# Scores of three batches from float16 halves, and a plain float32 mix over the sequence, in an attention and mixer kernel

## The chip, the cores and the metric

The kernel runs on one core of a Trainium2 chip. Its time is the device time of one execution in microseconds. Before the change the median of three runs is 691.39 us (687.16 to 692.56).

## What is computed

The reference is attention with rotary positions followed by a mixer, for 4 batches, 8 heads, 576 positions and 64 numbers a head:

```python
q_rot, k_rot = (rotate(q), rotate(k))
scores = scale * np.matmul(q_rot, k_rot.transpose(0, 1, 3, 2))
scores = scores - np.max(scores, axis=-1, keepdims=True)
attn = np.exp(scores)
attn = attn / (np.sum(attn, axis=-1, keepdims=True) + 1e-09)
x = np.matmul(attn, v)            # heads side by side: (4, 576, 512)
h = x.transpose(0, 2, 1) @ U @ V  # over the sequence: 576 -> 32 -> 576
u = x + h.transpose(0, 2, 1)
out = u + np.maximum(u @ w_ch1, 0.0) @ w_ch2   # 512 -> 2048 -> 512
```

All arrays are float32.

## The kernel before

Heads are taken in pairs (`hp`, four of them a batch): a pair's 2 x 64 numbers fill the 128 rows of a tile. For each pair `load_qk` (L814) fetches q and k, each with a copy whose halves are swapped, into one of three `raw` buffers, and `rope` (L823) multiplies by the tables `cs` or `csq` and adds the two parts into a float32 tile of `qk_ring`.

A pair has five tiles of scores (`score_tiles`, L844). In the first four, 128 positions of each of the two heads are multiplied with all 576 keys: the two heads lie on rows 0 to 63 and 64 to 127, so that each head's matmul uses one half of TensorE's rows, and the four matmuls (two heads, two stretches of 288 keys) stand in one group. The fifth tile takes the last 64 positions of both heads at once from `ql`, a tile with zeros outside the two diagonal blocks, and uses all 128 rows. There are two score buffers, `s0` and `s1`, of two PSUM banks each.

`softmax_tile` (L870) takes the minimum of the negated scores on DVE (`nb`), the exponential on ACT, and for all but two pairs of batch 0 a high float16 half `p16` on ACT and a low one on POOL, which a transfer transposes into `pt`. `values` (L910) multiplies these with the float16 halves of v (`vh`, `vl`, `vb`), divides by the sum (`xt`), transposes into `x`, and for batches 1 to 3 splits the tile into two rounded parts, `xh` (a copy, then a subtraction).

When two pairs are done, `mix` (L989) forms U^T x: for batches 1 to 3 as ten float32r matmuls of `ust` with the two parts of `xh`, for batch 0 as five plain float32 matmuls of `uf` with the tiles `xfs`. Then it multiplies by V and adds to `x`.

The mixer (`mlp`, L1210) of batch b runs beside the attention of batch b + 1. But for the first half of batch 0, both its products are float16: for each of two halves of the positions 192 matmuls `mm<-u,wt` and 192 `mm<-room,wt`, in two PSUM banks; ACT and DVE split the hidden values into float16 halves in `room`. The mixer of batch 3 is left for the end.

The order of all this is not the order of the code. Every call is a node of `Plan`, which knows what it reads and writes; `cost` (L127) prices a call, `place` chooses an engine where a call has several ways, and `schedule` lays the nodes out forward and backward and keeps the shortest layout. The instructions are emitted in that order, so each engine's queue is fixed when the kernel is built.

## Time and profile before

| | us |
|---|---|
| median of three runs | 691.39 |
| lowest and highest | 687.16, 692.56 |
| profiled execution | 687.07 |
| its span, first to last instruction | 685.3 |
| PE busy in the span | 646.4 |
| DVE busy | 407.1 |
| ACT busy | 365.9 |
| POOL busy | 268.4 |

PE is TensorE's matmuls, PEld its weight loads, DVE VectorE, ACT ScalarE, POOL GpSimd and SP the queue of the transfers. The profile shows one execution; its time is shorter than the median of the runs. Names such as `mm<-u,wt` tell the tile written and the tiles read. All instructions are emitted from one line (L310), so the groups are told apart by tiles. A float32 matmul has two records in the trace. The duration of a matmul is that of one in a pipeline: where matmuls follow each other, the time from one start to the next is shorter than the duration, and the chain gives such stretches.

### The profile page before, as it was taken

The page shows a single profiled execution, that of the slowest core. Times are in us where ns is not written, and L with a number is a line of the kernel's source. Part 1 is how long each engine was busy: PE and PEld are TensorE (multiplying, and loading weights), DVE is VectorE, ACT ScalarE, POOL GpSimd, SP SyncE. Part 2 cuts the span into 40 slices and gives each one's busy share as a digit, 9 for nine tenths or more (in the row PEclk, how much of TensorE's full clock was granted, in tenths as well). Part 3 has the DMA queues.
Part 4 walks back from the last instruction along what each step waited for, and adds up shares of the span by engine and source line. Part 5 has one row for each costly group of instructions (what it writes and reads, how often), then busy time and mean ns, then how long its engine had stood idle before and what let it go on. Part 6 is the DMA issues. An engine that isn't in the chain of part 4 may idle for free.

```text
span 685.3 us, 14779 instructions
## 1 busy us (share of the span) xinstructions
PE 646.4 (94%) x5792; PEld 489.4 (71%) x5792; DVE 407.1 (59%) x1031; ACT 365.9 (53%) x817; POOL 268.4 (39%) x220
## 2 busy tenths in 40 slices
PE   2799986999998999999999999999999999999998
PEld 1577764677766677776777777777777777777776
DVE  4989777878887755656645663665555553430210
ACT  3766564449889766437644764447545652220210
POOL 1411356113447766565447545256444341000000
PEclk9999699999999999999999999999999999999999
DMA  7979889275377567447765576166854463000000
GB/s 227 327 242 295 238 153 175 88 226 143 99 162 129 123 107 149 100 122 167 172 104 142 103 160 113 57 167 112 140 96 80 87 114 62 18 1 27 10 10 27
DMA packets 178342, 86.90 MB, mean 127 GB/s; under 512 B 152032, under 2 KB 167520, under 8 KB 178272
## 3 DMA queue, kind: packets, MB, share of 16 engines
q1 hardware_dynamic: 178272, 85.96, 54.2%
q8 instruction: 45, 0.74, 0.4%
q14 instruction: 25, 0.20, 0.1%
HBM read 41.70 MB, written 4.72 MB: 68 GB/s over the span
## 4 chain that ended last, share of the span: by engine, by line
PE 74%; DVE 8%; DMA 6%; ACT 5%; POOL 3%; issue 3%; SPq 0%; POOLq 0%; ACTq 0%; DVEq 0%
PE mm L310 53%; PE s L310 13%; PE pv L310 8%; DMA pt<-p 5%; DVE wt L310 3%; ACT junk L310 2%; DVE junk L310 2%; ACT p L310 1%; POOL raw L310 1%; POOL p L310 1%; DMA cs<-tab 1%; DVE rs L310 1%; DMA raw<-qk 1%; ACT wt L310 1%; ACT room L310 1%
## 5 line engine op out<-in xcount | busy, mean ns | idle before, releaser
L310 PEld LDWEIGHTS <-wt 128*128 128x128 f16 x2688 | 257.0, 98 | 75.3 <-issue 12.7
L310 POOL TENSOR_TENSOR p<-p,p 128x576 f16<-128x576 f32 x120 | 162.0, 1365 | 162.3 <-ACT p L310 112.4
L310 PE MATMUL mm<-room,wt 128*128 128x288 f16 (+1 forms) x1472 | 213.9, 297 | 0.0
L310 PE MATMUL mm<-u,wt 128*128 128x288 f16 x1344 | 180.9, 286 | 3.1 <-DVE room L310 3.0
L310 DVE TENSOR_SCALAR_CACHE_REDUCE junk<-s 128x576 bf16<-128x576 f32 x144 | 104.9, 752 | 62.0 <-PE s L310 59.6
L310 ACT ACTIVATE p<-s,nb 128x576 f32<-128x576 f32 x144 | 103.2, 740 | 47.7 <-DVE junk L310 45.0
L310 ACT ACTIVATE room<-mm 128x288 f16<-128x288 f32 (+3 forms) x139 | 56.5, 411 | 111.8 <-PE mm L310 111.0
L310 PE MATMUL s<-qk,qk 64*128 64x288 f32 x512 | 87.7, 452 | 11.1 <-DVE qk L310 10.9
L310 DVE SCALAR_TENSOR_TENSOR room<-mm,room 128x288 f16<-128x288 f32 x112 | 50.7, 455 | 74.6 <-ACT room L310 73.8
L310 PEld LDWEIGHTS <-pt 128*128 128x128 f16 x1722 | 66.4, 98 | 26.5 <-DMA pt<-p 13.3
L310 ACT ACTIVATE p<-p 128x576 f16<-128x576 f32 x120 | 78.9, 682 | 4.1 <-DMA pt<-p 3.5
L310 PEld LDWEIGHTS s<-qk,qk 64*128 64x128 f32 x512 | 49.7, 196 | 30.8 <-DVE qk L310 10.9
L310 PE MATMUL pv<-vh,pt 128*128 128x65 f16 (+2 forms) x600 | 58.8, 204 | 4.5 <-DMA pt<-p 4.3
L310 PE MATMUL pv<-vl,pt 128*128 128x64 f16 (+2 forms) x600 | 58.4, 204 | 0.0
L310 ACT ACTIVATE xt<-pv,rc 128x64 f32<-128x64 f32 (+1 forms) x99 | 26.7, 311 | 57.5 <-DVE rc L310 52.2
L310 DVE SCALAR_TENSOR_TENSOR ob<-mm,so,x 128x288 f32<-128x288 f32 x28 | 14.4, 516 | 45.1 <-PE mm L310 45.1
L310 PE MATMUL mm<-x,wt 128*128 128x288 f32 x128 | 34.8, 423 | 1.9 <-ACT room L310 1.1
L310 PE MATMUL pv<-vb,pt 128*128 128x65 f16 (+1 forms) x448 | 33.3, 197 | 0.1
L310 DVE SCALAR_TENSOR_TENSOR wt<-wt 128x512 int32<-128x512 int32 x46 | 33.2, 755 | 0.0
L310 POOL TENSOR_TENSOR raw<-raw,csq 128x1152 f32<-128x1152 f32 x9 | 24.5, 2728 | 21.0 <-DMA raw<-qk 9.5
L310 DVE TENSOR_SCALAR rs<-pv,sc_v 128x2 f32<-128x2 f32 x63 | 13.8, 218 | 30.2 <-PE pv L310 29.5
L310 PEld LDWEIGHTS mm<-x,wt 128*128 128x128 f32 x128 | 23.9, 194 | 9.8 <-DVE x L310 1.5
(149 smaller groups left out, 673.3 us busy)
## 6 DMA issues: line engine op xcount, KB each, us to landing
raw<-qk SPq DMA_DIRECT2D x30, 576.0 KB, 4.3
wt<-w SPq DMA_DIRECT2D x23, 512.0 KB, 4.8
out_t<-ob SPq DMA_DIRECT2D x32, 144.0 KB, 1.8
x<-w SPq DMA_DIRECT2D x6, 512.0 KB, 4.3
raw<-vt SPq DMA_DIRECT2D x6, 512.0 KB, 4.1
pt<-p SPq DMA_TRANSPOSE x120, 3.3
vb<-vh SPq DMA_DIRECT2D x6, 264.0 KB, 3.3
u<-w SPq DMA_DIRECT2D x3, 512.0 KB, 3.5
```

The lines of the kernel that those rows point to most:

```text
L310: getattr(getattr(nc, eng), op)(*a, **k)
```

## The change

For batches 1 to 3 (`b >= FB`), `half_scales` finds for each head pair a power of two for q and one for k from their sums of squares, and `rope` writes each scaled tile as a high and a low float16 half into the bytes where the float32 tile stood. `score_tiles` adds three products (high x high, high x low, low x high) in PSUM, still with two heads on the two halves of the rows. `softmax_tile` undoes the scales: in the minimum, in `nb` and in the exponential's scale, which now come from memory. `mix` uses the plain float32 matmuls of batch 0 for all batches, and `values` writes the tiles `xfs` at once; `ust` and `xhs` go. `cost` prices a group of twelve float16 matmuls on 64 rows at half.

```diff
 class Plan.cost
-                    us += max(m, 64) * (4 if a[2].dtype == F32R and m < 256 else 1) / 2400
+                    k = 2 if list(a[1].ap)[0][1] <= 64 and len(calls) == 12 else 1
+                    us += max(m, 64) * (4 if a[2].dtype == F32R and m < 256 else 1) / 2400 / k
...
+    ql_ring = cycle([cst.tile([P, 2, P], F16, name=f"qh{i}") for i in range(2)])
...
-    ust = cst.tile([P, NC, 4 * R], F32R, name="ust")
-    uf = carve(NC * 4 * R, F32).rearrange("p (c r) -> p c r", c=NC)
-    xfs = [carve(2 * P, F32).rearrange("p (c d) -> p c d", c=2) for t in range(NC)]
+    uf = cst.tile([P, NC, 4 * R], F32, name="uf")
+    xfs = [cst.tile([P, 2, P], F32, name=f"xf{t}") for t in range(NC)]
-    xhs = [cst.tile([P, 2, 2, P], F32R, name=f"xh{t}") for t in range(NC)]
...
+        if b >= FB:
+            half_scales(b, hp)
+
+    def half_scales(b, hp):
+        sq = tmp("sqk", [2], 2, "")
+        for x in (1, 0):
+            nc.scalar.activation(
+                out=junks[2], in_=state[b, hp]["raw"][x][:, 0], func=AF.Square,
+                accum_out=sq[:, x:x + 1],
+            )
+        pb = bank("")
+        nc.tensor.matmul(pb[:, 0:2], ones, sq, start=True, stop=True)
+        a = tmp("aqk", [2], 2, "")
+        nc.vector.tensor_scalar(
+            out=a.bitcast(I32), in0=pb[:, 0:2].bitcast(I32), scalar1=24, scalar2=23,
+            op0=ALU.logical_shift_right, op1=ALU.logical_shift_left,
+        )
+        inv, sc = tmp("iqk", [2], 2, ""), tmp("cqk", [2], 2, "")
+        nc.vector.tensor_scalar(
+            out=inv, in0=a, scalar1=2.0**-126, scalar2=2.0**(64 - 15), op0=ALU.max, op1=ALU.mult,
+        )
+        nc.vector.reciprocal(out=sc, in_=inv)
+        both = tmp("bqk", [3], 2, "")
+        for o, x, f in ((0, inv, 1.0), (1, inv, -1.0), (2, sc, LOG_PSC)):
+            nc.vector.tensor_scalar(
+                out=both[:, o:o + 1], in0=x[:, 0:1], scalar1=x[:, 1:2], scalar2=f,
+                op0=ALU.mult, op1=ALU.mult,
+            )
...
     def rope(b, hp, x):
...
+        if b >= FB:
+            sc = state[b, hp]["sc"][0][:, x:x + 1]
+            two(r[:, 0], r[:, 0], r[:, 1], ALU.add, "DP")
+            hi, lo = [qk_[x].bitcast(F16)[:, i * S:(i + 1) * S] for i in range(2)]
+            nc.scalar.activation(out=hi, in_=r[:, 0], func=AF.Copy, scale=sc)
+            scaled_low(lo, r[:, 0], sc, hi, "DP")
...
+            return
         two(qk_[x], r[:, 0, :], r[:, 1, :], ALU.add, "DP")
...
     def score_tiles(b, hp, t):
...
+                with nc.group():
+                    for j, (x, y) in enumerate(((0, 0), (0, 1), (1, 0))):
+                        for n in range(2):
+                            hs = slice(n * HS, (n + 1) * HS)
+                            for e, s in enumerate(ss):
+                                own = slice(0, P) if t == NT else slice(e * 64, e * 64 + 64)
+                                nc.tensor.matmul(
+                                    half(s, n),
+                                    lw[:, x] if t == NT else qw[own, x, t * P:(t + 1) * P],
+                                    kw[own, y, hs], start=j == 0, stop=j == 2,
+                                )
...
     def softmax_tile(b, hp, s, dst, sm):
...
-                    out=next(unread) if len(parts) == 1 else next(unread)[:, 0], in0=i, scalar1=0.0 if plain else LOG_PSC, scalar2=None,
+                    out=next(unread) if len(parts) == 1 else next(unread)[:, 0], in0=i,
+                    scalar1=sc[:, 2:3] if sc is not None else 0.0 if plain else LOG_PSC, scalar2=None,
                     op0=ALU.add, op1=ALU.min, accum_out=o,
...
+            down = -1.0
+            if sc is not None:
+                down = sc[:, 1:2]
+                scaled(nb[0], nb[0], sc[:, 0:1], "DP")
...
-                nc.scalar.activation(out=o, in_=i, func=AF.Exp, bias=nb[0], scale=-1.0, **more)
+                nc.scalar.activation(out=o, in_=i, func=AF.Exp, bias=nb[0], scale=down, **more)
...
-            xt = xfs[t][:, hp % 2] if FP and b == 0 else tmp("xt", [P], 2, "")
+            xt = xfs[t][:, hp % 2]
...
-            if not FP or b:
-                copy(xh[:, 0], xt[0:n], "ADP")
-                two(xh[:, 1], xt[0:n], xh[:, 0].bitcast(F32), ALU.subtract, "DP")
...
-                    for k in range(2):
-                        nc.tensor.matmul(
-                            hold["t1"][:, 0:256], ust[:n, t, :],
-                            xhs[t][:n, k].rearrange("p c d -> p (c d)"),
-                            start=(t == 0 and k == 0), stop=(t == NT and k == 1),
-                        )
+                    nc.tensor.matmul(
+                        hold["t1"][:, 0:256], uf[:n, t, :],
+                        xfs[t][:n].rearrange("p c d -> p (c d)"),
+                        start=(t == 0), stop=(t == NT),
+                    )
```

The planner lays everything out anew, so rows far from the change move too. Three places show the pattern. On PE, a group of scores of a pair tile in batch 2, before and then after (the first seven of its rows; `qk1_0` holds q, `qk1_1` k):

```order
L310 MATMUL mm2_66<-ident_69,xt0_134 128x128
L310 MATMUL s1_62<-qk1_1_78,qk1_0_77 128x288
L310 MATMUL s0_61<-qk1_1_78,qk1_0_77 128x288
L310 MATMUL s1_62<-qk1_1_78,qk1_0_77 128x288
L310 MATMUL s0_61<-qk1_1_78,qk1_0_77 128x288
L310 LDWEIGHTS pt_92
L310 MATMUL pv_63<-vh_83,pt_92 128x2x65
```

On PE after, from the mixer's matmul ahead of such a group:

```order
L312 MATMUL mm0_64<-u_104,wt_82 128x288
L312 LDWEIGHTS qk1_0_77
L312 MATMUL s1_62<-qk1_1_78,qk1_0_77 128x288
L312 LDWEIGHTS qk1_0_77
L312 MATMUL s0_61<-qk1_1_78,qk1_0_77 128x288
L312 LDWEIGHTS qk1_0_77
L312 MATMUL s1_62<-qk1_1_78,qk1_0_77 128x288
```

Four float32 matmuls have become twelve float16 ones that alternate between the two heads, each with a row of its own for the weight load (the order has none for float32).

On PE, the last mix of batch 3, before:

```order
L310 MATMUL s0_61<-xh0_97,ust_81 128x256 x2
L310 MATMUL s0_61<-xh1_98,ust_81 128x256 x2
L310 MATMUL s0_61<-xh2_99,ust_81 128x256 x2
L310 MATMUL s0_61<-xh3_100,ust_81 128x256 x2
L310 MATMUL s0_61<-xh4_101,ust_81 128x256 x2
```

And after:

```order
L312 MATMUL s0_61<-xf0_85,uf_84 128x256
L312 MATMUL s0_61<-xf1_86,uf_84 128x256
L312 MATMUL s0_61<-xf2_87,uf_84 128x256
L312 MATMUL s0_61<-xf3_88,uf_84 128x256
L312 MATMUL s0_61<-xf4_89,uf_84 128x256
```

Ten matmuls have become five.

On DVE, in the attention of batch 2, the minima of two score tiles, before:

```order
L310 TENSOR_SCALAR junk0_119,nb_124<-s1_62 128x576
L310 TENSOR_SCALAR junk1_120,nb_124<-s0_61 128x576
L310 TENSOR_SCALAR rs_130<-pv_63,sc_v_129 128x2
L310 RECIPROCAL rc_131<-rs_130 128x2
L310 SCALAR_TENSOR_TENSOR room_73<-mm1_65,room_73 128x288
```

And after, where the scale of the next pair (`aqk`, `iqk`, `cqk`) and its low halves stand in the same queue:

```order
L312 TENSOR_SCALAR aqk_138<-mm2_66 128x2
L312 SCALAR_TENSOR_TENSOR room_73<-mm1_65,room_73 128x288
L312 TENSOR_SCALAR iqk_139<-aqk_138 128x2
L312 RECIPROCAL cqk_140<-iqk_139 128x2
L312 SCALAR_TENSOR_TENSOR room_73<-mm0_64,room_73 128x288
L312 TENSOR_SCALAR junk0_121,nb_127<-s1_62,bqk_141 128x576
L312 TENSOR_SCALAR junk1_122,nb_127<-s0_61,bqk_141 128x576
L312 SCALAR_TENSOR_TENSOR room_73<-mm1_65,room_73 128x288
L312 TENSOR_SCALAR nb_127<-nb_127,bqk_141 128x1 x2
L312 SCALAR_TENSOR_TENSOR qk1_1_78<-raw0_100,cqk_140,qk1_1_78 128x576
L312 SCALAR_TENSOR_TENSOR qk1_0_77<-raw1_101,cqk_140,qk1_0_77 128x576
```

Each minimum reads a pointer (`bqk`) and is followed by a scaling of `nb`, here with one of the mixer's subtractions between them.

Over the whole program the order counts, before and after: on DVE 0 and 92 scalings of `nb` (POOL has 16 more), 0 and 24 low halves, 13 and 23 rope products, 35 and 0 subtractions for `xh`; on ACT 0 and 24 squares, 0 and 24 high halves, 126 and 18 exponentials with a constant scale, 28 and 0 copies for `xh`; on SP 270 and 270 instructions.

## Rows read from the trace of the kernel before

**Rows 1.** Stretches of the span: us from:to, length, busy us of each engine (instructions)

```profile
0.00:120.00 120.00, 94.77 (x724) 71.56 (x724) 95.40 (x230) 69.54 (x174) 41.25 (x43) 0.91 0.88 237
120.00:285.00 165.00, 158.11 (x1291) 116.09 (x1291) 124.99 (x293) 117.97 (x252) 80.78 (x62) 1.00 0.60 137
285.00:431.00 146.00, 144.07 (x1465) 109.22 (x1464) 81.00 (x227) 80.90 (x176) 81.24 (x63) 1.00 0.61 131
431.00:577.00 146.00, 145.12 (x1472) 109.92 (x1472) 78.77 (x224) 81.01 (x179) 65.18 (x52) 1.00 0.52 104
577.00:685.30 108.30, 104.29 (x845) 82.64 (x844) 26.97 (x60) 16.45 (x38) 0.00 (x0) 1.00 0.04 15
```

**Rows 2.** Waits of PE: in total, times, longest

```profile
PE s L310 <- DVE qk L310: 10.9, 1, 10.9
PE pv L310 <- DMA pt<-p: 4.3, 9, 1.1
```

**Rows 3.** The chain that ended last: start us, us, what, records

```profile
322.32 1.17 PE s L310 x8
...
332.84 1.10 PE pv L310 x28
...
355.69 0.98 PE s L310 x4
...
588.52 46.59 PE mm L310 x378
```

**Rows 4.** Groups of instructions, weight loads of the mixer: busy us, mean ns | idle before

```profile
L310 PEld LDWEIGHTS <-wt 128*128 128x128 f16 x2688 | 257.0, 98 | 75.3 <-issue 12.7
```

**Rows 5.** The chain, the mix over the sequence: batch 0's second, then first and last of six

```profile
120.70 2.35 PE s L310 x10
...
227.42 1.38 PE s L310 x10
...
576.81 1.56 PE s L310 x10
```

**Rows 6.** Timeline of PE at 440 us: start us, us, instruction

```profile
440.52 0.28 PE L310 MATMUL mm<-amv,ones 128*128 128x1 f32 x2
440.66 0.53 PE L310 MATMUL mm<-u,wt 128*128 128x288 f16 x3
```

**Rows 7.** Groups of instructions, ACT

```profile
L310 ACT ACTIVATE p<-p 128x576 f16<-128x576 f32 x120 | 78.9, 682 | 4.1 <-DMA pt<-p 3.5
...
L310 ACT ACTIVATE junk<-wt 128x512 bf16<-128x512 f32 x32 | 20.1, 627 | 0.7
...
L310 ACT ACTIVATION_READ_ACCUMULATOR junk<-wt 128x1 f32 x32 | 6.0, 188 | 0.0
...
L310 ACT ACTIVATE xh<-xt 128x128 fp32r<-128x128 f32 x21 | 6.5, 309 | 0.4
...
L310 ACT ACTIVATE u<-x,sck_u 128x576 f16<-128x576 f32 x6 | 4.4, 776 | 2.9 <-DVE sck_u L310 2.9
```

**Rows 8.** Groups of instructions, DVE

```profile
L310 DVE TENSOR_TENSOR qk<-raw 128x576 f32<-128x576 f32 x20 | 15.1, 757 | 0.4 <-POOL raw L310 0.3
...
L310 DVE TENSOR_SCALAR rs<-pv,sc_v 128x2 f32<-128x2 f32 x63 | 13.8, 218 | 30.2 <-PE pv L310 29.5
...
L310 DVE TENSOR_TENSOR xh<-xt,xh 128x128 fp32r<-128x128 f32 x25 | 10.7, 427 | 6.8 <-ACT xh L310 6.1 <-POOL xh L310 0.4
...
L310 DVE TENSOR_TENSOR raw<-raw,cs 128x1152 f32<-128x1152 f32 x7 | 9.5, 1356 | 0.0
...
L310 DVE SCALAR_TENSOR_TENSOR u<-x,sck_u,u 128x576 f16<-128x576 f32 x6 | 5.0, 848 | 0.6 <-ACT u L310 0.6
```

**Rows 9.** Stretches of the span in batch 1

```profile
160.00:180.00 20.00, 19.60 (x132) 14.31 (x131) 16.79 (x31) 18.77 (x43) 7.92 (x7) 1.00 0.55 143
180.00:200.00 20.00, 18.78 (x142) 13.53 (x140) 17.60 (x36) 17.99 (x34) 6.60 (x6) 1.00 0.52 111
200.00:220.00 20.00, 19.66 (x186) 13.98 (x185) 14.42 (x44) 18.51 (x39) 13.70 (x13) 1.00 0.64 135
```

More of the change, by code (lines that the diff above doesn't have):

```diff
@@ L28 @@
 PAIR0 = 0
-FP = 1
 PLH = 1
@@ L37 @@
 SKEW = 1
+FB = 1
 class Plan:
@@ L587, in prep_uv @@
         single((ur[:, 0:NT], ud[:, 0:NT]), (ur[0:REM, NT], ud[0:REM, NT]), (vr, vd))
+        fill(uf[:, :, 3 * R:4 * R], 0.0)
         for n, cc in ((P, slice(0, NT)), (REM, slice(NT, NC))):
             for i in range(3):
-                copy(ust[:n, cc, i * R:(i + 1) * R], ur[:n, cc, :], "ADP")
-            two(ust[:n, cc, 3 * R:4 * R], ur[:n, cc, :], ust[:n, cc, 0:R].bitcast(F32),
-                ALU.subtract, "DP")
-        if FP:
-            fill(uf[:, :, 3 * R:4 * R], 0.0)
-            for n, cc in ((P, slice(0, NT)), (REM, slice(NT, NC))):
-                for i in range(3):
-                    copy(uf[:n, cc, i * R:(i + 1) * R], ur[:n, cc, :], "ADP")
+                copy(uf[:n, cc, i * R:(i + 1) * R], ur[:n, cc, :], "ADP")
         copy(vst, vr, "ADP")
@@ L628, in tile_rope_attention_then_mixer @@
     scales = {}
-    junks = [cst.tile([P, S], BF16, name=f"junk{i}") for i in range(2)]
+    junks = [cst.tile([P, S], BF16, name=f"junk{i}") for i in range(3)]
     junk = junks[0][:, 0:DM]
-    unread = cycle(x.rearrange("p (a b) -> p a b", a=2) for x in junks)
+    unread = cycle(x.rearrange("p (a b) -> p a b", a=2) for x in junks[:2])
     def weight(g):
@@ L821, in load_qk @@
         state[b, hp]["raw"] = raws
+        if b >= FB:
[25 more added lines that the diff above has]
+            )
+        state[b, hp]["sc"] = sc, both
+        ql = state[b, hp]["ql"] = next(ql_ring)
+        if b == FB and hp < 2:
+            fill(ql[0:64, :, REM:P], 0.0)
+            fill(ql[64:P, :, 0:REM], 0.0)
     def rope(b, hp, x):
@@ L834, in rope @@
             two(r, r, c, ALU.mult, "DP")
+        if b >= FB:
[4 more added lines that the diff above has]
+            scaled_low(lo, r[:, 0], sc, hi, "DP")
+            if not x:
+                l = state[b, hp]["ql"]
+                for e in range(2):
+                    own = slice(e * 64, e * 64 + 64)
+                    i = qk_[0].bitcast(F16).rearrange("p (w s) -> p w s", w=2)
+                    copy(l[own, :, e * REM:(e + 1) * REM], i[own, :, MAIN:S], "APD")
+            return
         two(qk_[x], r[:, 0, :], r[:, 1, :], ALU.add, "DP")
@@ L849, in score_tiles @@
             ss, mm = [], []
+            if b >= FB:
+                qw, kw = [
+                    i.bitcast(F16).rearrange("p (w s) -> p w s", w=2) for i in (qn, kn)
+                ]
+                lw = state[b, hp]["ql"]
+                ss = [scores(b) for _ in range(1 if t == NT else 2)]
+                with nc.group():
[9 more added lines that the diff above has]
+                                )
+                return ss
             if t == NT:
@@ L880, in softmax_tile @@
             nb = [tmp("nb", [1], 4, "") for _ in parts]
+            sc = state[b, hp]["sc"][1] if b >= FB else None
             for o, (i, _) in zip(nb, parts):
                 nc.vector.tensor_scalar(
-                    out=next(unread) if len(parts) == 1 else next(unread)[:, 0], in0=i, scalar1=0.0 if plain else LOG_PSC, scalar2=None,
+                    out=next(unread) if len(parts) == 1 else next(unread)[:, 0], in0=i,
+                    scalar1=sc[:, 2:3] if sc is not None else 0.0 if plain else LOG_PSC, scalar2=None,
                     op0=ALU.add, op1=ALU.min, accum_out=o,
                 )
+            down = -1.0
+            if sc is not None:
+                down = sc[:, 1:2]
+                scaled(nb[0], nb[0], sc[:, 0:1], "DP")
             if len(nb) > 1:
@@ L973, in turn @@
                 begun.add(hp if 1 else 9)
-            xh = xhs[t][0:n, :, hp % 2]
             tp = bank(f"tp{b}_{hp}_{t}")
@@ L1000, in project @@
                     n = P if t < NT else REM
-                    if FP and b == 0:
-                        nc.tensor.matmul(
-                            hold["t1"][:, 0:256], uf[:n, t, :],
-                            xfs[t][:n].rearrange("p c d -> p (c d)"),
-                            start=(t == 0), stop=(t == NT),
-                        )
-                        continue
-                    for k in range(2):
-                        nc.tensor.matmul(
-                            hold["t1"][:, 0:256], ust[:n, t, :],
-                            xhs[t][:n, k].rearrange("p c d -> p (c d)"),
-                            start=(t == 0 and k == 0), stop=(t == NT and k == 1),
-                        )
+                    nc.tensor.matmul(
[3 more added lines that the diff above has]
+                    )
         def parts():
```

## The prediction

> **What bounds the kernel now.** I read the stages first. The windows by stage [rows 1] cut the span at the ends of the four attention passes: batch 0 (0 to 120 us), then batch 1 beside the mixer of batch 0 (to 285), batch 2 beside the mixer of batch 1 (to 431), batch 3 (to 577), and a tail of mixer work alone. In the second and third of the changed stages PE is busy 144 and 145 of 146 us, with DVE and ACT at 79 to 81. There PE is the bound with room on every other engine. In batch 1 PE is busy 158 of 165, and DVE (125) and ACT (118) are near it. The waits of PE [rows 2] say the same from the other side: the longest single one, 10.9 us, is the start of the program, and the next kind, the wait for a transposed tile, is 4.3 us in nine pieces. So a microsecond taken from PE in batches 1 to 3 is a microsecond of the end, unless another engine comes late, and I price the change by PE's rows.
>
> The granted clock is 1.00, so 2.4 GHz, from 120 us on [rows 1]. Batch 0 (0.91 on average) is not touched except for the set-up of U, where some small copies go; I count that as nothing.
>
> **The pair groups of the scores (48 of them: 3 batches, 4 head pairs, 4 row tiles).** Before, one group is four float32 matmuls, two heads on the two halves of the rows; the trace has two records for a float32 matmul, and the chain gives 1.17 us for the eight [rows 3]. The order shows twelve float16 matmuls of the same 288 columns in their place. A full-array float16 matmul of 288 columns with its own weight load takes 46.59/378 = 0.123 us in the tail [rows 3]. That bounds the group from both sides: 12 x 0.123 = 1.48 us if the two halves don't overlap at all (48 x 0.31 = 14.9 us lost), and half of it, 0.74, if they overlap fully (48 x 0.43 = 20.6 gained). The row between is the float32 pair itself: the tile with both heads' last rows uses the whole array and takes 0.98 us for four records [rows 3], 0.245 each, so eight in sequence would be 1.96 and the pair's 1.17 is 0.60 of that, not 0.50. At that share the float16 group takes 0.88 (13.9 gained). I take 0.80, nearer to full overlap, for this reason: 28 of the values' float16 matmuls, each with a load, pass in 1.10 us [rows 3], 0.039 each, so two loads need under 0.08 us of the 0.123 that a pair of matmuls streams, and don't bind. Gain 0.37 x 48 = **17.8 us**.
>
> The Trainium skill, in "TensorE: Matmul & The Clock Gate" (Part 3, What overlaps and what doesn't), says that a weight load overlaps matmuls in flight only where it goes to another row group. The tail disagrees for the whole array: there every matmul has its load on the same rows, the loads last 98 ns on the mean [rows 4], and the matmuls still follow at 123 ns, where 288 columns at 2.4 GHz take 120. By that rule a load on one half would wait for that half's own matmul; by the tail it would not. For half arrays in float16 no run here shows it, so it is the slower rival below.
>
> **The last tiles (12).** Two float32 matmuls on the whole array, 0.98 us [rows 3], become six float16 ones: 6 x 0.123 = 0.74. Gain 0.24 x 12 = **2.9 us**.
>
> **The mix over the sequence (6: two for each of batches 1 to 3).** Before, ten matmuls of rounded halves; the first of the six takes 1.38 us and the last 1.56 [rows 5], I use 1.45. After, five plain float32 ones, of which batch 0 has the row already: 2.35 us for ten records [rows 5]. Loss 0.90 x 6 = **5.4 us**. What this buys are the 60 copies and 60 subtractions on DVE, ACT and POOL that made the halves; they lie beside PE.
>
> **The scale of each head pair (12).** Each adds a matmul of ones with two columns. Such a matmul with one column holds PE from 440.52 to 440.66, 0.14 us, and lasts 0.28 [rows 6]. Between these I take 0.2: **2.4 us** lost (1.7 to 3.4).
>
> PE together: -17.8 - 2.9 + 5.4 + 2.4 = -12.9 us; from -16.4 (full overlap, cheap ones) to +20.8 (no overlap).
>
> **What lies beside PE.** ACT gets 24 squares with their sums (0.63 for 512 columns, some 0.68 for 576, and 0.19 for the sum: 20.9 us), 24 high halves (0.78, the row with a scale from memory: 18.6) and a scale from memory in 108 exponentials (0.78 against 0.68 without: 10). It loses 28 copies of halves (0.31: 8.7) [rows 7], and the copies of the last rows change by little: about +39 us, 13 a batch. DVE gets 24 low halves (0.85: 20.4), 92 scalings of a row minimum and 72 small steps of the scale (0.22 at most: 36), a pointer in 108 minima (0.85 - 0.76 = 0.09, by the rows with and without one: 10) and, by the order, 10 rope products that POOL did (1.36: 13.6). It loses 35 subtractions (0.43: 15) [rows 8], and casts that I leave unpriced. That is at most +65 us, 22 a batch. SP issues as many instructions as before, 270. The tiles of the normalised values go straight into the mix's operand, one write as before. In batches 2 and 3 ACT then stands at 94 and DVE at no more than 103 of some 142 us, so this work is covered by PE.
>
> In the queues, the scaling of the minimum stands between the minimum and the exponential; behind it wait the exponential, the tile's transposition, and the next group that wants the score bank. A small step of 0.2 us in a chain that has 7.3 us a tile (146/20) moves nothing on PE while the mixer's matmuls stand between. The scale chain itself (squares, matmul of ones, three steps, product, two halves) lengthens the way from a landed transfer to the first scores by some 4 us, and a head pair's transfers are asked for at the second of the five tiles of the pair before, some 4 x 7.3 = 29 us ahead.
>
> In batch 1 the cover is thin: from 160 to 220 us ACT is busy 18.8, 18.0 and 18.5 of each 20 [rows 9], with DVE at 14 to 18. Between nothing and the whole 13 us of ACT's new work, I charge 2.5 us.
>
> **The sum.** The profiled execution took 687.07 us (span 685.3 and 1.8 around it). -12.9 + 2.5 = -10.4, so 676.7 beside it, or 0.985. The median of the runs, 691.39, is 4.3 above that execution. On it the change gives **681.0 us**.
>
> **Rivals.**
> Partial overlap: the halves overlap only as well as the float32 ones did, 0.88 us a group. Then the gain is 13.9 and the sum -13.9 - 2.9 + 5.4 + 2.4 + 2.5 = -6.5: 684.9, just inside 1%. For it: it is the only overlap this trace shows. Against: float32 loads are dearer than the float16 ones of the values' rows. The Trainium skill ("TensorE: Matmul & The Clock Gate", Part 3, Measured speedup vs the span model) gives 3.07 times for four row tiles; an estimate from that share, 1.53 times for two, would make a group 0.96 us and the time 688.8, and no run here shows such a group.
>
> Slower: the load on a half waits for the matmul on the same half. Then six rounds of 0.123 + 0.098 [rows 3, 4] make a group 1.33 us, 48 x 0.16 = 7.7 lost, and the sum is 7.7 - 2.9 + 5.4 + 2.4 + 2.5 = +15.1: 706. It decides from a group of 1.01 us on (no gain left) and costs over 1% from 1.16 on. For it: the twelve matmuls alternate between two halves, so each load has its own half's matmul just ahead. Against: the tail's 123 ns. This is also the case in which the change does not do what it says.
>
> Another bound in batch 1: ACT's new 13 us fall where ACT had 4.7 us left in 60 [rows 9]. The stage then ends 8.3 late and its third of PE's gain (4.3) is idle: -12.9 + 4.3 + 8.3 = -0.3, so 691. With all 13 late it is +4.4, 696. For it: the 90% rows. Against: the weights' conversion fills ACT there, and the attention of batch 1 runs on to 285, where ACT has a quarter free.
>
> **How the numbers follow.** A measurement of this kernel tells about 1% from no change (its runs spread from 687.16 to 692.56). Forecast 0.64 (0.57 of it over 1% faster, the rest in the upper part of its spread, up to 687), partial overlap 0.12 (0.03 and 0.09), load on the half 0.09 (all slower), batch 1 bound 0.15 (0.02 faster, 0.09 same, 0.04 slower). That is faster 0.62, same 0.25, slower 0.13. The range goes from full overlap with nothing late (691.4 - 16.4 = 675, less 4 for the low end of the runs: 671) to batch 1's worst, 696; the loads' case stays out.
>
> **What would show it.** Right: pair groups of twelve at 0.74 to 0.85 us, last tiles at 0.74, mixes at 2.3 us, and stages 2 and 3 shorter by 4 to 5 us each with PE still over 98% busy. Wrong: groups over 1 us; PE waiting for ACT's or DVE's `room` or for `p`, the tile with the exponentials, in batch 1; a stage 2 in which DVE or ACT stands over 90%.

## The result, and the profile after

The changed kernel takes 696.25 us (median of 20 runs, 694.0 to 704.27); the kernel before, run beside it, 691.69 (20 runs, 687.15 to 697.51). The ratio is 1.0091 with a 95% interval of 1.0069 to 1.0114. The forecast was 681.0, faster, from 671 to 696: wrong in its direction, and just outside its range. The interval lies above 1, so the change is a loss, of some 0.9%.

First the stages, cut at the start of the last mix of each batch (as in [rows 1]: from and to, length, busy us of PE, PEld, DVE, ACT and POOL, each with its instructions, then the granted clock, the DMA share and GB/s; batch 0, batch 1, batch 2, batch 3, tail). After:

```profile
0.00:117.00 117.00, 91.26 (x725) 69.86 (x726) 94.26 (x242) 69.80 (x170) 32.26 (x40) 0.94 0.89 243
117.00:292.50 175.50, 160.31 (x1395) 119.74 (x1396) 141.56 (x351) 129.33 (x260) 59.09 (x48) 0.97 0.60 127
292.50:437.80 145.30, 139.19 (x1527) 106.74 (x1526) 95.99 (x262) 96.63 (x199) 69.11 (x59) 1.00 0.66 130
437.80:583.20 145.40, 140.77 (x1544) 108.06 (x1544) 92.03 (x256) 89.70 (x183) 63.32 (x54) 1.00 0.56 108
583.20:692.60 109.40, 105.43 (x846) 83.05 (x845) 26.97 (x60) 16.47 (x38) 0.00 (x0) 1.00 0.04 15
```

The same cuts in the kernel before, for batches 1, 2 and 3:

```profile
120.70:285.40 164.70, 158.18 (x1293) 116.09 (x1292) 124.31 (x289) 117.81 (x251) 80.78 (x62) 1.00 0.60 137
285.40:431.30 145.90, 143.97 (x1465) 109.07 (x1463) 81.00 (x226) 80.75 (x176) 81.24 (x63) 1.00 0.61 131
431.30:576.80 145.50, 144.62 (x1470) 109.53 (x1469) 78.74 (x223) 80.86 (x178) 65.18 (x52) 1.00 0.53 104
```

The span grew by 7.3 us: batch 0 -3.7, batch 1 +10.8, batch 2 -0.6, batch 3 -0.1, tail +0.9. These are single executions; the one of the kernel before was 4.6 us under its median and the one of the changed kernel 2.0, which is why the span grew by more than the median (4.6). Read the length and PE's busy time together. In batches 2 and 3 PE lost 4.8 and 3.9 us of busy time, 8.6 together, and the forecast has two thirds of 12.9, which is 8.6. But PE's idle time (length less busy) grew from 1.9 to 6.1 and from 0.9 to 4.6, so almost nothing of it reached the end. In batch 1 the idle time grew from 6.5 to 15.2, busy time grew too, and the mean clock is 0.97.

The stages do not hold quite the same work, though. The planner moved 23 of the mixer's float16 matmuls `mm<-room,wt` from batches 2 and 3 into batch 1: 136 of them begin in batch 1 before and 159 after, and the rows by groups below show the same 23, as 764 and 741 in batches 2 and 3. At the tail's 0.123 us each that is an estimated 2.8 us. So for the same work batch 1 is some 8.0 us longer, not 10.8, batches 2 and 3 together are 2.1 us longer, not 0.7 shorter, and PE's loss of busy time in them is some 5.8 us, not 8.6.

The chain that ended last, pieces of the new kernel: a group of twelve, another one, the six matmuls of a last tile, a mix (compare [rows 3, 5]):

```profile
149.43 0.89 PE s L312 x12
...
187.52 0.84 PE s L312 x12
...
237.87 2.35 PE s L312 x10
...
480.16 0.90 PE s L312 x6
```

Of the 14 whole groups among the longest pieces of the chain nine take 0.84 us, four 0.89 to 0.91 and one 1.07, so mostly 0.84 to 0.91 where 0.80 was forecast and 1.17 stood before. A mix takes 2.35, as forecast. The last tile has 0.90 here, counted to the end of its last matmul, where 0.74 was forecast; what it saves is read better from busy time. The groups of PE over batches 2 and 3 give the same in busy time, after:

```profile
L312 PE MATMUL mm<-room,wt 128*128 128x288 f16 x741 | 104.8, 286 | 0.0
...
L312 PE MATMUL s<-qk,qk 64*128 64x288 f16 x384 | 29.7, 284 | 1.0 <-ACT p L312 1.0
...
L312 PE MATMUL s<-qk,qh 128*128 128x288 f16 x48 | 7.2, 286 | 0.6 <-ACT p L312 0.6
...
L312 PE MATMUL mm<-sqk,ones 128*128 128x2 f32 x14 | 2.1, 217 | 0.0
```

and before:

```profile
L310 PE MATMUL mm<-room,wt 128*128 128x288 f16 x764 | 103.5, 286 | 0.0
...
L310 PE MATMUL s<-qk,qk 64*128 64x288 f32 x256 | 39.7, 429 | 0.0
...
L310 PE MATMUL s<-qk,ql 128*128 128x288 f32 x32 | 9.1, 406 | 0.0
```

Two batches have 32 pair groups and 8 last tiles. The pair groups lost 10.0 us, 0.31 each (forecast 11.9), the last tiles 1.9, 0.24 each (forecast 1.9), and the matmuls of ones cost at most 2.1 (forecast 1.6).

The waits of PE (compare [rows 2]):

```profile
PE pv L312 <- DMA pt<-p: 9.9, 12, 2.4
PE s L312 <- ACT p L312: 5.8, 7, 1.5
PE mm L312 <- DVE room L312: 5.0, 8, 1.5
PE mm L312 <- ACT xf L312: 3.3, 5, 1.2
```

The wait for transposed tiles rose from 4.3 to 9.9 us, and the three kinds behind it rose too (they were 3.6, 3.0 and, for the tile that is now `xf`, 1.6 us). None is the one late transfer or engine that one would look for: they are a few tenths to 2.4 us each, at the ends of chains that run over ACT, POOL, the transfers and DVE.

The new work beside PE, by groups:

```profile
L312 ACT ACTIVATE p<-s,nb,bqk 128x576 f32<-128x576 f32 x108 | 88.6, 827 | 24.0 <-DVE nb L312 18.5 <-POOL p L312 3.8 <-PE pv L312 1.2
...
L312 DVE SCALAR_TENSOR_TENSOR qk<-raw,cqk,qk 128x576 f16<-128x576 f32 x24 | 22.9, 960 | 0.4 <-ACT qk L312 0.4
L312 DVE TENSOR_SCALAR nb<-nb,bqk 128x1 f32<-128x1 f32 x92 | 19.3, 212 | 2.2
L312 ACT ACTIVATE qk<-raw,cqk 128x576 f16<-128x576 f32 x24 | 18.3, 770 | 10.9 <-DVE cqk L312 6.5 <-DVE raw L312 4.4
...
L312 ACT ACTIVATE junk<-raw 128x576 bf16<-128x576 f32 x24 | 16.3, 678 | 8.2 <-DMA raw<-qk 8.2
```

The sizes were right: 0.68 for a square, 0.77 for a high half (0.78 forecast), 0.21 for a scaling of a minimum (0.22 at most), 0.83 for an exponential with a scale from memory (0.78); a low half took 0.96 (0.85). Over the span ACT went from 365.9 to 401.9 (+36; forecast +39, though the terms listed there add up to 41) and DVE from 407.1 to 450.8 (+44; forecast at most +65). The first row also shows where the new step stands: the exponentials waited 18.5 us in all for DVE's scaled minima. That is no new waiting of ACT. Before, the 144 exponentials waited 45.0 us for the minima themselves; after, these 108 and the 36 of batch 0 wait 29.3 us for DVE (18.5 and 10.8):

```profile
L310 ACT ACTIVATE p<-s,nb 128x576 f32<-128x576 f32 x144 | 103.2, 740 | 47.7 <-DVE junk L310 45.0 <-POOL room L310 1.0 <-POOL p L310 0.8
```

### The profile page after: what moved, and what is told of

Read it like the earlier page. It is cut to its first block, busy times and chain, and to the rows that moved or that the text cites. A ratio compares the mean times of both kernels' runs of the same rounds, so it can differ in the third digit from the quotient of the medians.

```text
span 692.6 us, 15423 instructions
## 1 busy us (share of the span) xinstructions
PE 637.0 (92%) x6032; PEld 487.4 (70%) x6032; DVE 450.8 (65%) x1170; ACT 401.9 (58%) x849; POOL 223.8 (32%) x200
## 4 chain that ended last, share of the span: by engine, by line
PE 65%; DMA 12%; DVE 11%; ACT 6%; issue 3%; POOL 2%; SPq 1%; ACTq 0%; POOLq 0%; DVEq 0%
PE mm L312 48%; PE s L312 11%; DMA pt<-p 9%; PE pv L312 6%; ACT p L312 3%; DMA raw<-qk 3%; DVE junk L312 3%; DVE raw L312 2%; POOL p L312 1%; DVE wt L312 1%; DVE qk L312 1%; ACT junk L312 1%; DVE room L312 1%; POOL raw L312 1%; ACT xf L312 1%
## 5 line engine op out<-in xcount | busy, mean ns | idle before, releaser
L312 POOL TENSOR_TENSOR p<-p,p 128x576 f16<-128x576 f32 x120 | 159.0, 1335 | 207.6 <-ACT p L312 174.6
L312 PE MATMUL mm<-room,wt 128*128 128x288 f16 (+1 forms) x1472 | 217.4, 298 | 0.0
L312 DVE TENSOR_SCALAR_CACHE_REDUCE junk<-s,bqk 128x576 bf16<-128x576 f32 x108 | 87.3, 811 | 33.2 <-PE s L312 27.3
L312 ACT ACTIVATE p<-s,nb,bqk 128x576 f32<-128x576 f32 x108 | 88.6, 827 | 24.0 <-DVE nb L312 18.5
L312 PEld LDWEIGHTS <-pt 128*128 128x128 f16 x1722 | 69.7, 99 | 26.9 <-DMA pt<-p 17.7
L312 PE MATMUL s<-qk,qk 64*128 64x288 f16 (+1 forms) x704 | 70.1, 323 | 13.2 <-DVE qk L312 10.8
L312 ACT ACTIVATE xf<-pv,rc 128x64 f32<-128x64 f32 (+1 forms) x106 | 28.5, 309 | 40.3 <-DVE rc L312 36.6
L312 PEld LDWEIGHTS <-qk 64*128 64x128 f16 x576 | 25.7, 95 | 17.0 <-issue 12.1
L312 ACT ACTIVATE p<-s,nb 128x576 f32<-128x576 f32 x36 | 26.0, 736 | 12.4 <-DVE junk L312 10.8
L312 DVE TENSOR_SCALAR_CACHE_REDUCE junk<-s 128x576 bf16<-128x576 f32 x36 | 25.9, 753 | 8.7 <-PE s L312 8.1
```

The source lines that it names most:

```text
L312: getattr(getattr(nc, eng), op)(*a, **k)
```

## Where batch 1 lost its time

Four stretches of batch 1 of the changed kernel, columns as above:

```profile
207.00:217.00 10.00, 7.98 (x97) 5.67 (x96) 9.33 (x23) 9.04 (x23) 4.44 (x3) 1.00 0.39 77
217.00:224.40 7.40, 4.50 (x56) 3.49 (x55) 7.40 (x16) 6.29 (x11) 2.91 (x2) 1.00 0.63 119
224.40:234.60 10.20, 7.45 (x56) 5.10 (x56) 7.09 (x24) 8.71 (x21) 3.57 (x4) 0.50 0.78 175
234.60:240.00 5.40, 4.89 (x38) 3.78 (x36) 3.34 (x7) 3.55 (x9) 2.65 (x3) 0.99 0.37 59
```

In the second, DVE is busy for all of 7.40 us and PE for 4.50. Then the granted clock is 0.50, which is 1.2 of 2.4 GHz, for 10.2 us: what PE still does there takes about twice as long, and only 56 matmuls pass. The timeline shows what stood in front (start, us, instruction, idle before it and what ended it; pieces of several engines):

```profile
217.71 0.68 ACT L312 ACTIVATE p<-p 128x576 f16<-128x576 f32 x1
...
218.50 2.38 DVE L312 SCALAR_TENSOR_TENSOR wt<-wt,sck_b 128x1024 f16<-128x1024 f32 x1
218.52 1.28 POOL L312 TENSOR_TENSOR p<-p,p 128x576 f16<-128x576 f32 x1 [2.39 <-ACT p L312]
...
220.91 1.15 ACT L312 ACTIVATE wt<-wt,sck_b 128x1024 f16<-128x1024 f32 x1 [1.08 <-DVE wt L312]
...
221.97 1.24 ACT L312 ACTIVATE p<-p 128x576 f16<-128x576 f32 x2
222.27 1.27 DVE L312 SCALAR_TENSOR_TENSOR wt<-wt,sck_b 128x1024 f16<-128x1024 f32 x1
...
223.06 0.20 PE L312 MATMUL pv<-vh,pt 128*128 128x65 f16 x1 [2.37 <-DMA pt<-p]
...
224.48 0.81 ACT L312 ACTIVATE p<-s,nb,bqk 128x576 f32<-128x576 f32 x1
...
225.34 1.59 PE L312 MATMUL s<-qk,qk 64*128 64x288 f16 x11 [1.47 <-ACT p L312]
```

A low half of the mixer's weights on DVE takes 2.38 us; ACT's next piece of the weights waits 1.08 us for it, the float16 copies of two tiles `p<-p` stand behind that piece in ACT's queue, and behind them the exponential at 224.48, for which PE then waits 1.47 us. The chain that ended last runs this way, from DVE's piece at 218.50 to the group at 225.34. PE's other wait, 2.37 us for a transposed tile, is of an earlier tile: its low half on POOL, at 218.52, came after ACT's copy at 217.71. The last line is a group at the lower clock: 1.59 us for eleven matmuls, where twelve take 0.84. The weights were converted in batch 1 before the change as well; what is new is that DVE and ACT hold more of other work between them. That this queue is the cause is read from this one trace, and the experiments test it.

## Experiments

All ratios are to the kernel before, run beside each, with 95% intervals; the two columns of stages are lengths in us, cut as above, from each run's profile. The last column counts the float16 matmuls `mm<-room,wt` in batch 1, which the planner moves between the stages. "For the same work" below means batch 1 shortened, and batches 2 and 3 lengthened, by 0.123 us (an estimate, from the tail's pace) for each such matmul that was moved into batch 1 from them, and the other way round where fewer are in batch 1. A stage's length is that of one execution, and the profiled ones lie from 7.2 us below their kernels' medians to 4.7 above; batch 0, in one and the same order, took 117.0, 118.8, 121.6 and 125.6 us in four of them.

| run | median (runs) | ratio | batch 1 | batches 2 + 3 | `room,wt` |
|---|---|---|---|---|---|
| before | 691.69 (20) | | 164.7 | 291.4 | 136 |
| after | 696.25 (20) | 1.0091 [1.0069, 1.0114] | 175.5 | 290.7 | 159 |
| mix_only | 696.33 (10) | 1.0115 [1.0072, 1.0159] | 166.4 | 298.3 | 131 |
| scores_only | 698.5 (4) | 1.013 [1.0073, 1.0186] | 178.3 | 290.9 | 158 |
| from_batch_2 | 686.73 (10) | 0.9956 [0.991, 1.0002] | 166.3 | 288.8 | 134 |
| unscaled_halves | 687.23 (10) | 0.9955 [0.9917, 0.9992] | 166.7 | 289.0 | 134 |
| less_pe_same_order | 684.36 (4) | 0.9894 [0.9848, 0.994] | 170.5 | 279.5 | 159 |
| less_side_same_order | 690.54 (10) | 0.9977 [0.9946, 1.0009] | 174.1 | 287.2 | 159 |
| less_weight_squares | 694.7 (10) | 1.006 [1.0025, 1.0096] | 174.4 | 291.7 | 159 |
| unscaled_late | 698.16 (4) | 1.0104 [1.0051, 1.0157] | 177.1 | 290.3 | 134 |
| unscaled_late_old_mix | 688.58 (10) | 0.9951 [0.9919, 0.9983] | 174.5 | 279.4 | 147 |
| before_relaid | 693.7 (10) | 1.0044 [1.0012, 1.0077] | 171.4 | 290.3 | 137 |
| after_relaid | 703.24 (4) | 1.0187 [1.0111, 1.0263] | 180.1 | 289.6 | 157 |
| unscaled_old_mix | 683.87 (7) | 0.9895 [0.9853, 0.9937] | 170.0 | 282.7 | 147 |
| unscaled_old_mix_relaid | 685.53 (9) | 0.9926 [0.9889, 0.9962] | 172.2 | 282.2 | 146 |
| rope_on_pool | 702.32 (6) | 1.0138 [1.0087, 1.019] | 179.0 | 289.0 | 183 |

**The two parts apart.** `mix_only` is the changed kernel with float32 scores in all batches; `scores_only` has the scaled halves and the mix of before, for which the rings of `xt` and `ob` have two buffers and the last rows' halves lie in the bytes of `ql`.

```diff
 mix_only
-FB = 1
+FB = 4
 scores_only
-            xt = xfs[t][:, hp % 2]
+            xt = xfs[t][:, hp % 2] if FP and b == 0 else tmp("xt", [P], 2, "")
...
+                copy(xh[:, 0], xt[0:n], "ADP")
+                two(xh[:, 1], xt[0:n], xh[:, 0].bitcast(F32), ALU.subtract, "DP")
```

> The plain float32 mix for all batches, with the scores of before (FB = 4). Side-work theory (the changed kernel loses PE's gain because ACT and DVE get 36 and 44 us of work for the scales and halves): PE gains 5.4 us of work, the side engines lose some 30 us, so 0 to +5 us over before, about 693 to 697, and no drop of the granted clock in batch 1. Mix theory (the longer mix and its operand tiles, which stay taken until it is done, are what costs): at least +8, over 699. Layout theory (any new layout of the planner moves the time by some microseconds): anywhere from -4 to +8.

> Scores of batches 1 to 3 from scaled float16 halves, with the mix of before (for room, the output staging and the xt ring have two buffers in place of three, and the last rows' halves lie in the bytes of ql). Side-work theory: PE loses some 17 us of work but ACT and DVE keep the copies and subtractions for the mix on top of the new work: the stage of batch 1 stays over 172 us, the time 690 to 698. Mix theory: without the longer mix the scores' gain shows, 674 to 682. Layout theory: anything between 683 and 698.

Each part alone is a loss. The mix costs what the forecast gave it or a little more (5.4 forecast, 1.0115 x 691.69 - 691.69 = 8.0 measured, 5.0 to 11.0), and its stages are longer in batches 2 and 3, by 6.3 us for the same work: PE's busy time rose there by 4.1 (3.6 forecast) and its idle time by 2.2, where the wait for DVE's `room` grew from 0.9 to 2.9. The scores, which were to bring 18 us, bring nothing in batches 2 and 3 here, where the mean clock is 0.98, and make batch 1 13.6 us longer, 10.9 for the same work. Its clock shows the same picture as the changed kernel's, a stretch in which PE is half idle and then the lower clock:

```profile
205.00:215.00 10.00, 5.35 (x78) 3.98 (x76) 8.97 (x17) 8.11 (x20) 1.69 (x2) 0.97 0.46 92
214.50:221.30 6.80, 6.25 (x48) 4.06 (x45) 6.77 (x19) 5.36 (x12) 3.58 (x5) 0.50 0.52 133
```

**Without the halves in batch 1, and without the scales.** `from_batch_2` takes the halves for batches 2 and 3 alone. `unscaled_halves` drops the scales (squares, sums, steps, pointers, scalings of the minima) and splits the unscaled float32 tile; its range is then that of float16, which the scales were to guard.

```diff
 from_batch_2
-FB = 1
+FB = 2
 unscaled_halves
-            sc = state[b, hp]["sc"][0][:, x:x + 1]
...
-            nc.scalar.activation(out=hi, in_=r[:, 0], func=AF.Copy, scale=sc)
-            scaled_low(lo, r[:, 0], sc, hi, "DP")
+            copy(hi, r[:, 0], "A")
+            two(lo, r[:, 0], hi, ALU.subtract, "DP")
...
-            sc = state[b, hp]["sc"][1] if b >= FB else None
+            sc = None
```

> The whole change, but the scores of batch 1 stay float32 (FB = 2). Side-work theory: batch 1, where ACT and DVE were near full beside the weights, gets its 164 to 168 us back and the clock stays at 1.00; batches 2 and 3 give their 145 as in the changed kernel, so 686 to 692. Mix theory: the stage of batch 1 stays over 172, time about 695. Layout theory: 686 to 698.

> The whole change, but the float16 halves are made of the unscaled float32 values: no squares, no matmul of ones, no scale steps, no scaling of the row minima, and constants again in the minima and exponentials. PE has the same work but for the 12 matmuls of ones; ACT is relieved of some 26 us, DVE of some 40. Side-work theory: PE's gain now shows: 676 to 684, stages of batches 2 and 3 at 141 to 143. Mix theory: no better than 690. Layout theory: 685 to 698.

Both are some 9 us faster than the changed kernel, and batch 1 is back at 166.3 and 166.7. So in these layouts the loss goes when either the scaled halves of batch 1 or their scales go. `unscaled_late` below, which has no scales and no halves in batch 1 and was expected at 681 to 686, yet took 698.16, shows that two layouts are not enough to say so.

**Less work in the same order.** Here the order is that of the changed kernel, instruction by instruction. `less_pe_same_order` issues only the product high x high and leaves out the two with a low half. `less_side_same_order` leaves out the scalings of `nb`, takes a constant in the minima and squares 64 of 576 columns. `less_weight_squares` squares 64 of 512 columns of the weights on ACT.

```diff
 less_pe_same_order
+            keep = {12: 4, 6: 2}.get(len(calls)) if calls[0][1] == "matmul" else None
-            for eng, op, a, k in self.chosen[n]:
+            for eng, op, a, k in calls[:keep]:
 less_side_same_order
+                if op == "tensor_scalar" and out.tensor.name == in_.tensor.name == NB[0]:
+                    continue
...
+                if op == "activation" and k["out"].tensor.name == NB[1]:
+                    k = dict(k, out=k["out"][:, 0:64], in_=k["in_"][:, 0:64])
 less_weight_squares
+                if op == "activation" and k["in_"].tensor.name == NB[0] and k["func"] == AF.Square:
+                    k = dict(k, out=k["out"][:, 0:64], in_=k["in_"][:, 0:64])
```

> The changed kernel in its own order of instructions, but of each score group of batches 1 to 3 only the product of the two high halves is issued (the two products with a low half are left out). PE has some 31 us less to do and nothing else changes. If PE is what sets the end of the stages, the time falls by about that, to 665. Side-work theory: batch 1 stays within 5 us of its 175 and batches 2 and 3 give at most 3 each: 685 to 692.

> The changed kernel in its own order of instructions, but the row minima are not rescaled (no scaling of nb, and a constant in the minima), and the squares read 64 of the 576 columns. PE has the same work; DVE has some 27 us less, ACT 10. Side-work theory: the stage of batch 1 falls by 6 to 10 us from 175, without the drop of the granted clock; batches 2 and 3 by 1 to 3 each: 682 to 689. If PE sets the end, no change: 694 to 697.

> The changed kernel in its own order, but the 32 squares of the weights, all in batch 1, read 64 of 512 columns (so the weights' scale comes from an eighth of them). ACT has 12 us less to do between 140 and 240 us, nothing else changes. If batch 1 is held up by ACT's queue, the stage falls from 175 to 170 or less and the clock does not drop: 686 to 691. If not, 694 to 697.

With two thirds of the scores' matmuls gone (batches 1, 2, 3):

```profile
125.60:296.10 170.50, 150.25 (x1250) 110.95 (x1250) 141.65 (x351) 128.53 (x260) 61.46 (x48) 0.98 0.60 130
296.10:436.00 139.90, 130.32 (x1384) 98.88 (x1383) 94.76 (x262) 95.88 (x199) 69.53 (x59) 1.00 0.69 136
436.00:575.60 139.60, 132.60 (x1401) 99.85 (x1400) 90.42 (x256) 89.42 (x184) 63.38 (x54) 1.00 0.60 112
```

PE loses 10.1, 8.9 and 8.2 us of busy time, and the stages 5.0, 5.4 and 5.8. So in this order about 0.6 of a microsecond taken from PE reaches the end, in batches 2 and 3 too (12 to 14 of 27 us by the median and the ratio, a little less); the rest turns into idle time, though in batches 2 and 3 DVE and ACT are busy for two thirds of the stage only. The time, 684.36, is just under the side-work theory's range (685 to 692) and far from the 665 of a kernel that PE alone bounds. The side work taken away gives 1.4 us in batch 1 and 3.5 in batches 2 and 3; the time falls by 5.7 by the median (690.54 for 696.25) and by 7.9 by the ratio. So this part of the scales' side work costs the changed kernel 5 to 8 us, no less than the whole change lost (4.6 by the median, 6.3 by the ratio), and since the order is the same, a new layout has no part in it. The time lies between the two ranges (682 to 689 for the side-work theory, 694 to 697 where PE sets the end), and batch 1 gave less than that theory's 6 to 10. Besides, 11 us less of ACT in batch 1 (129.3 to 118.2) give 1.1. That is the answer to the rival of the forecast in which ACT's throughput bounds batch 1: it does not.

**The layout.** A nudge of the planner (48 for 50 in two places of its due times) lays the same work out anew; `unscaled_late` and `unscaled_late_old_mix` take unscaled halves from batch 2 on, with either mix, so that batch 1 holds float32 scores.

```diff
-        with plan.sooner(20 if b == 0 else 50):
+        with plan.sooner(20 if b == 0 else 48):
```

> The kernel before, with the planner's head start for the score groups of batches 1 to 3 at 48 nodes in place of 50: the same work in another layout. If the layout alone moves the time, this lies 3 us or more from the 691 of before, and the stage of batch 1 lies between 165 and 178. If the stage lengths follow from the work, 689 to 693 and 163 to 167.

> The changed kernel with the same nudge of the planner (48 in place of 50). If the loss in batch 1 is an accident of this layout, the stage falls to some 166 us without a drop of the clock, and the time to 684 to 690. If it follows from the work, 694 to 699 and a stage of 172 to 178.

> Unscaled float16 halves for the scores of batches 2 and 3 alone, batch 1's scores as before, and the plain mix. Against the run with the old mix PE has 5.4 us more and the side engines some 30 us less. Side-work theory: batch 1 at 165 to 168, batches 2 and 3 at 142 to 144: 681 to 686. Layout theory: 684 to 696.

> Unscaled float16 halves for the scores of batches 2 and 3 alone, batch 1 as before, and the mix of before (the halves of the last rows lie in the bytes of ql, the xt ring has two buffers). PE saves some 6 us in each of batches 2 and 3 and loses none to the mix. Side-work theory: batch 1 at 164 to 167 us, batches 2 and 3 at 140 to 143: 677 to 682, faster than both kernels. Layout theory: 684 to 696.

Both kernels lose by the nudge, the changed one more than either theory gave it (0.4% and 1.0% by the ratios), and in the profiles batch 1 carries it: 164.7 to 171.4 for before, 175.5 to 180.1 for after. The change costs batch 1 8.0 us for the same work in the one layout and 6.2 in the other. But the same kind of work in batch 1 has given very different lengths: float32 scores with the plain mix 166.4, 166.3 and 177.1, with the old mix 164.7, 171.4 and 174.5. In `unscaled_late` one gap alone, in which PE waits for DVE's `gt` (an operand of the mix), is 4.3 us, and the clock is low behind it. All layouts together, for the same work: float32 scores six times, 164.7 to 177.3, mean 170.0; unscaled halves three times, 166.9 to 171.0, mean 168.9; scaled halves four times, 172.7, 173.2, 175.6 and 177.5, mean 174.7. So some 5 us on the mean go with the scales, but the two longest of the six with float32 scores (173.1 and 177.3) lie among the four. The whole times, which no moved work touches, say the same: the four with scaled halves in batch 1 have ratios of 1.009 to 1.019, the nine other layouts (1 for the kernel before) 0.990 to 1.012, two of them over 1.009. Besides, the kernel before, at 164.7, had the shortest batch 1 of all, 5 us under the mean of its kind. How much of that is its layout and how much the one execution that was profiled, 4.6 us under its median, no run here tells; the nudge cost its median 2.0 us, and 0.4% by the ratio.

**DVE's queue.** The planner had given 23 of 30 rope products to DVE (13 before). `rope_on_pool` gives those of batches 1 to 3 to POOL.

```diff
-            two(r, r, c, ALU.mult, "DP")
+            two(r, r, c, ALU.mult, "P" if b else "DP")
```

> The changed kernel with the products of the rope of batches 1 to 3 given to POOL alone (the changed order has 23 of 30 rope products on DVE, the order of before 13). All other work is the same, and the planner lays it out anew. Theory that DVE's queue makes batch 1 long (rope products of 1.3 us and weights' halves stand in front of the mixer's halves and the row sums): DVE loses some 13 us over the three batches, its stalls near 210 us go, batch 1 comes back from 175 to 165 to 168 us, and the time is 686 to 690. Rival, that the layout decides and that any engine's queue will do: batch 1 stays over 172 us, and the time is 694 to 700. Second rival: POOL, which also makes the low halves of the exponentials, is late for the transposed tiles, PE's waits for them grow from 9.9 us to over 15, and the time is 698 or more.

```profile
PE mm L312 <- DVE room L312: 10.8, 12, 2.1
...
115.90:294.90 179.00, 163.13 (x1420) 120.82 (x1421) 134.86 (x342) 130.18 (x263) 74.77 (x53) 0.98 0.56 124
```

DVE has 6.7 us less to do in batch 1, and batch 1 is 179.0, 173.2 for the same work as before against 172.7 in the changed kernel. The wait for DVE's `room` is twice as long, and the time is 702.32. The theory that the products on DVE make batch 1 long falls: it was the queue that the trace showed, but taking them out of it does not bring the time back. The second rival falls by its sign, PE's waits for transposed tiles, which fell from 9.9 to 2.8 us; the first came nearest, with a time over its range.

**The version that beats both.** Unscaled halves with the mix of before, and the same with the nudge. (Its diff is the one of `unscaled_halves` with the mix of `scores_only`; `ob` keeps three buffers.)

> Unscaled float16 halves in batches 1 to 3 and the mix of before. PE has 18 us less than before, the side engines some 12 us more. If PE sets the end in batches 2 and 3, they take 139 to 142 us each, as in the run that left batch 1 alone; batch 1 between 163 and 167 if its layout has no stall, else 172 to 176: 677 to 683, or 686 to 692.

> The version with unscaled float16 halves and the old mix, laid out anew by a nudge of the order (48 for 50 in the planner's two due times). Theory that its gain over the kernel before is the scores' work taken from PE, and the layout adds a few us of noise either way: 681 to 690, batches 2 and 3 again 139 to 143 us each. Rival, that 683.87 was a lucky layout: 691 to 698, with batches 2 and 3 at 145 or more.

Batches 1, 2 and 3 of `unscaled_old_mix`:

```profile
121.10:291.10 170.00, 158.32 (x1376) 116.96 (x1375) 129.05 (x293) 123.31 (x263) 75.66 (x60) 0.97 0.57 130
291.10:430.90 139.80, 137.18 (x1529) 105.12 (x1526) 86.30 (x233) 85.07 (x180) 90.84 (x72) 1.00 0.67 137
430.90:573.80 142.90, 138.21 (x1541) 106.38 (x1539) 79.01 (x227) 82.02 (x174) 76.51 (x62) 1.00 0.57 106
```

It is 1% faster than the kernel before (0.9895), and still 0.7% after the nudge, so the gain was not one lucky layout; the first time, 683.87, lies between the two ranges given for it, next to the lower one. In batches 2 and 3 the three layouts with unscaled halves and the old mix (`unscaled_late_old_mix` is the third) took 282.7, 282.2 and 279.4 against 291.4 and 290.3 with float32 scores. For the same work PE's busy time falls there by 11.8 us in `unscaled_old_mix` and the stages by 7.3, so here too about 0.6 of PE's gain reaches the end.

## Why the prediction was wrong, step by step

- **Pair groups.** Forecast 0.37 us a group, measured 0.26 to 0.33. The halves overlap, less than at 0.80: most groups lie between the forecast and the rival of partial overlap (0.88). For the 48 groups that is some 15 us by busy time (10.0 x 3/2), not 17.8. The slower rival, in which a load waits for the matmul on its own half (1.33 us), did not come: twelve matmuls, each with its load, passed in 0.84 us. The Trainium skill, "TensorE: Matmul & The Clock Gate", Part 3, What overlaps and what doesn't, states that a weight load overlaps matmuls in flight only on another row group; these groups do not agree with it, since every half has a matmul and a load of its own, of 95 ns on the mean, six times in 0.84 us.
- **Last tiles, mix, matmuls of ones.** Right: busy time of last tiles -1.9 for -1.9 in two batches, mix 2.35 for 2.35, matmuls of ones at most 2.1 for 1.6. PE's sum in batches 2 and 3 looks right to the tenth, 8.6 for 8.6, but that is luck: 2.8 of it is mixer work that moved into batch 1. For the same work it is 5.8, near what the groups add up to (-10.0 for the pair groups, -1.9 for the last tiles, +3.5 for the mix, +2.1 for the matmuls of ones, -6.3 together).
- **"So this work is covered by PE".** This step failed in batches 2 and 3. Its evidence was busy shares, DVE and ACT at two thirds of the stage, and those came out as forecast. But PE's idle time rose by 7.9 us in the two batches, more than the gain of 5.8 for the same work, and PE was busy for 96 and 97% of them where the prediction's sign asked for over 98. An engine that is busy for two thirds of a stage can still be late with the one instruction that PE waits for. `less_side_same_order` shows that the side work was not covered: without most of the scales' part of it these batches are 3.5 us shorter in the same order. And `less_pe_same_order` shows that PE was not alone the bound, as 0.6 of what it loses reaches the end.
- **"A microsecond taken from PE in batches 1 to 3 is a microsecond of the end, unless another engine comes late".** The condition holds the error: the prediction priced the engines' lateness by their totals and not by the chains.
- **The charge of 2.5 us for batch 1.** Too small: the stage was to be 1.8 us shorter (PE's gain of 4.3 less the charge) and was 10.8 longer, 8.0 for the same work. PE's idle time rose 8.7 us; its busy time, which should have fallen by the 4.3, rose by 2.1. The difference of 6.4 is the moved mixer work (2.8) and the lower clock: at 0.50 PE was busy for 7.45 us, about half of which (3.7, an estimate) the full clock would have saved. The rival "another bound in batch 1" gave 691 to 696 and comes nearest in number, but that is luck: it went by ACT's throughput, which `less_weight_squares` rules out. What is shown: most of the scales' instructions together cost 5 to 8 us in a fixed order, 1.4 of it in batch 1 (`less_side_same_order`). What is likely: with scaled halves batch 1 is some 5 us longer on the mean of four layouts, which overlap with the others. It comes neither with the halves alone nor from the rope products on DVE. Which of the scales' instructions does it, and how much of the rest of batch 1's loss is the layout, stays open.
- **"A small step of 0.2 us in a chain moves nothing on PE".** The step was 0.21 us. Without it, with a constant in the minima and with smaller squares, batches 2 and 3 were 3.5 us shorter in the same order; what the step alone costs was not tested.
- **The plain mix.** PE's price was right. That alone it made batches 2 and 3 some 5 to 6 us longer for the same work (6.3 and 4.7; 298.3 for 291.4 as measured, and 289.0 for 282.7 with unscaled halves), where PE's part is 4 x 0.9 = 3.6, was not foreseen. In `mix_only` the rest is idle time of PE, behind DVE's `room`; why that came later is open.
- **What was not considered:** that the kernel before may sit in a favourable layout, that a new layout alone moves batch 1 by 5 to 10 us, and that the planner can move work between the stages.

## What to carry to other kernels

Price a change that takes work from the bounding engine and gives it to its neighbours by the chains through the neighbours' queues, not by their busy shares: at two thirds busy they still made PE idle for longer than it had been relieved. Where a planner orders the program, lay out the kernel before anew by a nudge first; its spread (here 2 to 3 us in the time of one kernel and 7 in that of the other) is an error of any forecast made from one trace. Count the work in each stage before comparing stages. And test the expensive part and its safeguard apart: the float16 halves paid 1%, the scales that guard them and the plainer mix took 2% back.

## What was not expected of the hardware

- The granted clock fell to 0.50 after stretches in which PE was half idle, as in the rows of the changed kernel (PE 4.50 busy of 7.40 us, then 10.2 us at 0.50) and of `scores_only`. In every profile of the table but that of the kernel before the clock was at 0.50 for some of batch 1, 3 to 14 us in all; the three of 166 to 167 us had 3, 3 and 7. So a wait of PE can cost more than itself: in the changed kernel a group of eleven matmuls took 1.59 us there, where twelve take 0.84 at 1.00.
- DVE and POOL held each other up. The low half of weights that began at 218.50 on DVE took 2.38 us beside a POOL instruction of 1.28, and the same form at 222.27 took 1.27; there it is POOL that lasts longer, 3.66 us for two, 1.10 over twice 1.28. The low halves of q and k have a mean of 960 ns, and near there the one without POOL beside it took 0.81 and the one with it 1.58:

```profile
221.54 0.81 DVE L312 SCALAR_TENSOR_TENSOR qk<-raw,cqk,qk 128x576 f16<-128x576 f32 x1
...
222.77 3.66 POOL L312 TENSOR_TENSOR p<-p,p 128x576 f16<-128x576 f32 x2 [2.97 <-ACT p L312]
...
223.71 1.58 DVE L312 SCALAR_TENSOR_TENSOR qk<-raw,cqk,qk 128x576 f16<-128x576 f32 x1
```

  So in these rows each of the two engines was longer at its work while the other worked beside it. No run tests it by itself.
